# Two-pass feed-forward kernel behind windowed attention: 64-row matmul tiles for the later attention units, exponentials of the first batch from PSUM, and a new written order

## The chip, the cores and the metric

The kernel runs on one core of a Trainium2 chip. That core has five engines that run their own instruction streams and meet at semaphores: TensorE (PE, with its weight loads shown apart as PEld), VectorE (DVE), ScalarE (ACT), GpSimd (POOL) and SyncE (SP), whose queue issues nearly all of the DMAs here. The metric is the device time of one execution in microseconds. The kernel before takes 800.28 us, the median of three runs (800.1 to 801.37).

## What is computed

Four sequences of 576 tokens with 8 heads of 64 go through attention with a causal window: heads 0 to 3 see the last 32 tokens ("plain"), heads 4 to 7 every fourth of the last 128 ("dilated"). The result, 2304 tokens by 512, goes through a feed-forward layer and then through a second, gated one.

```python
rel = pos[:, None] - pos[None, :]
mask_plain = (rel >= 0) & (rel < window)
mask_dil = (rel >= 0) & (rel < window * dilation) & (rel % dilation == 0)
scores = np.where(masks[None, :, :, :], scores, -1000000000.0)
scores = scores - np.max(scores, axis=-1, keepdims=True)
attn = np.exp(scores)
attn = attn / (np.sum(attn, axis=-1, keepdims=True) + 1e-09)
...
h = x @ w_in                  # 512 -> 2048
x = (h - np.tanh(h)) @ w_out  # 2048 -> 512
a = x @ w1; b = x @ w2        # 512 -> 1024 each
out = (a * b @ w3) @ w_out2   # 1024 -> 1024 -> 512
```

Everything is float32. In the two feed-forward layers each operand is split into a high part of reduced precision (fp32r) and the rest, and three products of the parts make one product. The attention matmuls take float32 as it is; such a matmul stands in the trace as two records.

## The kernel before

**Units.** Attention is cut into 12 units: 4 batches times 3 groups of 3 query tiles of 64. A unit has two types, plain (`p`) and dilated (`d`), and a type has two pairs of heads; `e` is the pair, `h` the head within it. The tokens of the dilated heads are sorted by remainder on the host, so that both types see a band of 64 keys for each 32 queries. Units 0 to 2 are batch 0 ("first batch", `n < PB`); they go type by type. Units 3 to 11 are the later ones; their two types share one tile of two PSUM banks.

**Steps of a unit**, with the letters that the written order uses: `q` load keys and queries, `s` scores (`at_scores`, L508: a mask is laid into the bank by a bf16 matmul, L496, then 24 matmuls for each type contract all 128 rows, in which the queries of one head are followed by zeros for the other, into 32-partition strips), `M` maximum and subtraction on DVE (L526, L529), `E` exponential on ACT (L535), `N` sum and reciprocal on DVE (L541 to L546), `m` multiplication on POOL (L551), `T` three transposes for each type on PE (L561), `C` copies out of PSUM on ACT (L574: two for each type, each with a per-partition factor that keeps the rows of one head pair and zeroes the other's), `v` load values, `P` product with the values (`at_pv`, L592: 12 matmuls for each type, all 128 rows, 64 columns), `X` and `L` the high and low part into the activations X (ACT L614, DVE L619).

**The order.** `ORDER` is a table of words, one for each step of each unit, mixed with the steps of the first feed-forward group on a tile of tokens: `h` (L635), `t` tanh, `g`, `G`, `k` the split, `y` (L725), `Y` and `Z` evacuations; and with the preparation of weights: `w` load, `a`, `b`, `c` four bit operations that turn a float64 word into float32 (L144 on ACT; L149, L153, L159, L162 on DVE), `i`, `o` the split. The words are run through once and each engine gets its instructions in that order; nothing is reordered afterwards. Behind the table stand the other groups of the first layer, the second layer's weights and its products, none of which the change touches.

**Buffers.** The keys and queries of later units have three buffers each, one for a type of a unit; the values three; a weight waiting for conversion has two. A DMA on SP's queue is issued in the written order when its buffer is free and when the eighth DMA before it has landed.

Of the kernel before, what the change touches and what calls it, by code (L numbers as in the profile page):

```python
# [8 lines left out]
F32 = mybir.dt.float32  # L9
# [26 lines left out]
R = 4  # L36
# [13 lines left out]
K0 K1 q0p q1p s0p q2p q0d M0p q1d s1p E0p s2p s0d M1p N0p m0p w0 T0p E1p C0p N1p M2p q2d M0d E2p m1p  # L50
N2p T1p v0p s1d v1p m2p s2d w1 a0 E0d C1p T2p b0 P0p C2p N0d c0 M1d X0p M2d E1d v2p a1 m0d L0p b1
T0d q3p E2d P1p C0d w2 a2 q3d P2p N1d c1 m1d T1d s3 N2d C1d i0 m2d i1 T2d b2 c2 v0d v1d X1p L1p w3
P0d o0 X2p L2p o1 X0d i2 M3 P1d L0d X1d E3 a3 L1d q4p q4d h0 v2d s4 N3 C2d P2d w4 b3 t0 g0 h1 G0 c3
i3 X2d M4 t1 a4 m3p T3p k0 o2 L2d q5p E4 q5d g1 o3 y0 w5 h2 v3p q6p G1 s5 C3p v3d b4 c4 t2 k1 m3d
T3d g2 q6d i4 o4 a5 N4 C3d h3 m4p M5 t3 E5 b5 P3p c5 v4p T4p v4d C4p y1 N5 X3p L3p g3 P3d G2 X3d m4d
T4d i5 k2 C4d L3d s6 M6 q7p q7d o5 P4p v5p X4p L4p h4 t4 m5p y2 Y2 G3 E6 P4d X4d w6 g4 h5 T5p Z2 C5p
m5d s7 N6 G4 L4d v5d P5p k3 y3 t5 g5 a6 X5p G5 T5d C5d w7 k4 a7 b6 k5 v6p m6p L5p y4 h6 M7 q8p t6
T6p c6 g6 q8d y5 q9p C6p i6 h7 G6 v6d E7 b7 t7 c7 g7 P5d N7 k6 w8 G7 Y5 m6d s8 q9d X5d P6p X6p Z5
T6d k7 h8 v7p m7p y6 L5d C6d P6d t8 M8 a8 E8 g8 G8 q10p m7d h9 N8 m8p X6d v7d T7p C7p s9 T7d o6 k8
t9 g9 y7 C7d h10 M9 t10 L6p g10 T8p G9 v8p E9 i7 N9 b8 P7p L6d X7p w9 y8 h11 k9 m8d L7p Y8 q10d s10  # L60
q11p G10 t11 C8p m9p P7d g11 q11d Z8 X7d P8p X8p L7d L8p T8d k10 y9 G11 M10 h12 c8 y10 E10 k11 C8d
t12 v8d m9d v9p a9 v9d y11 w10 T9p C9p g12 h13 G12 P8d b9 Y11 k12 Z11 t13 N10 m10p g13 T9d m10d G13
s11 M11 P9p X8d L8d C9d X9p k13 c9 E11 y12 w11 T10p h14 y13 C10p T10d t14 g14 a10 b10 G14 P9d k14
N11 m11p L9p C10d v10p h15 t15 v10d y14 g15 G15 Y14 h16 v11p T11p t16 k15 Z14 g16 y15 X9d o7 L9d G16
k16 m11d P10p X10p h17 C11p c10 t17 v11d P10d g17 G17 y16 L10p X10d T11d C11d h18 a11 t18 P11p X11p
L10d L11p P11d k17 X11d w12 g18 y17 L11d Y17 b11 Q0 i8 G18 i9 c11 h19 Z17 k18 t19 o8 g19 h20 G19 h21
w13 t20 y18 k19 i10 y19 h22 g20 t21 g21 G20 G21 k20 i11 k21 y20 a12 h23 b12 o9 a13 b13 t22 g22 G22
o10 o11 Z20 k22 Y20 h24 c12 t23 c13 g23 i12 y21 G23 y22 o12 k23 i13 y23 t24 g24 G24 o13 k24 Z23 Y23
# [12 lines left out]
def attn_moe_kernel(  # L81
# [362 lines left out]
    def load_v(n, parts=AB):  # L444
        if n < NU:
            b, g = units[n]
            for ty in parts:
                v = v_home(n).rearrange("p (h t c) -> p h t c", h=2, t=TU)
                for e in range(2):

                    for t0, t1 in ((0, 1), (1, TU)) if g == 0 else ((0, TU),):
                        src = vt[b, 2 * ty + e, :HW, TU * g + t0:TU * g + t1].rearrange("k t c -> k (t c)")
                        ap = [list(d) for d in src.ap]
                        step = ap[0][0] * window(TU * g + t0, 1)
                        nc.sync.dma_start(
                            out=v[e:128:2, :, t0:t1].rearrange("k h t c -> k h (t c)"),
                            in_=bass.AP(tensor=src.tensor, offset=src.offset, ap=[ap[0], [step, 2], ap[1]]),
                        )
                vs[n, ty] = v
# [8 lines left out]
    def bank_of(n, ty):  # L468

        if n >= PB:  # L470
            return ust[n]["both"][:, ty]
# [706 lines left out]
```

## Time and profile before

| | |
|---|---|
| median of three runs | 800.28 us |
| profiled execution: own time | 802.01 us |
| its span, first to last instruction | 800.2 us |
| PE busy in the span | 779.9 us (97%) |
| DVE, ACT, POOL busy | 548.1, 292.8, 158.3 us |
| mean granted clock of TensorE | 0.994 |
| DMA, mean over the span | 144 GB/s; 298 GB/s in the first 37 us |

The profiled execution took 802.01 us and its instructions span 800.2 us of that. A busy PE is not PE at its peak: matmuls overlap in the array, so the duration of one record is longer than the distance between two. What a stretch of matmuls costs is read from the chain of work, where each piece lasts until the next one begins, and from counts of records in a window. The attention lies in the first 131 us; after that PE runs feed-forward matmuls until the end.

### The profile page before, as it was taken

The numbers are of one execution on the slowest core, as the hardware profiler recorded it, in microseconds if no ns is written. First come the engines' busy times: TensorE is split into PE (matmuls) and PEld (weight loads), VectorE is DVE, ScalarE is ACT, GpSimd is POOL, SyncE is SP. The second block draws the span as 40 slices with busy tenths as digits, with TensorE's granted clock in tenths as the row PEclk, the third lists the DMA queues.
The fourth block names the chain that finished last, engine by engine and source line by source line (L and its number), as shares of the span: only waits on it lengthen the run. The fifth ranks groups of instructions, "written<-read, shape, count | busy, mean of one in ns | idle before, by whom it ended". The sixth has DMA issues, their size and how long they took to land.

```text
span 800.2 us, 14174 instructions
## 1 busy us (share of the span) xinstructions
PE 779.9 (97%) x5592; PEld 688.0 (86%) x5592; DVE 548.1 (68%) x909; ACT 292.8 (37%) x546; POOL 158.3 (20%) x153
## 2 busy tenths in 40 slices
PE   5699999999999999999999999999999999999998
PEld 4589999888889888898888898799998999899996
DVE  4998675668888779987888889954454544734431
ACT  3566565443444444444444444321122111311111
POOL 3363343500022001210022223211121111211111
PEclk9799999999999999999999999999999999999999
DMA  9988742114455253632554344296203750156302
GB/s 300 302 247 294 236 155 73 53 53 126 150 160 158 105 162 116 186 119 66 156 155 136 105 134 131 93 340 211 93 1 115 238 187 1 41 181 202 118 1 79
DMA packets 62018, 115.58 MB, mean 144 GB/s; under 512 B 6400, under 2 KB 27008, under 8 KB 61952
## 3 DMA queue, kind: packets, MB, share of 16 engines
q1 hardware_dynamic: 61664, 114.32, 44.8%
q8 instruction: 44, 0.72, 0.4%
q10 hardware_dynamic: 288, 0.36, 0.2%
q14 instruction: 22, 0.18, 0.1%
HBM read 95.26 MB, written 19.40 MB: 143 GB/s over the span
## 4 chain that ended last, share of the span: by engine, by line
PE 89%; DVE 8%; ACT 1%; DMA 1%; issue 1%; ACTq 0%; SPq 0%; DVEq 0%
PE h L635 26%; PE y L725 25%; PE pr L979 22%; PE o L1042 6%; PE pr L1042 6%; PE x L592 2%; DVE a L159 2%; PE s L508 2%; DVE a L162 1%; DVE a L153 1%; PE t L561 1%; DVE a L149 1%; DVE Y L872 1%; DVE ms L541 1%; DMA id_sb<-in_ident 0%
## 5 line engine op out<-in xcount | busy, mean ns | idle before, releaser
L725 PE MATMUL y<-gs,LT 128*128 128x512 f32 (+1 forms) x520 | 121.9, 368 | 0.0
L725 PEld LDWEIGHTS y<-gs,LT 128*128 128x128 f32 x520 | 92.1, 188 | 16.3
L635 PE MATMUL h<-X,LT 128*128 128x512 f32 (+1 forms) x471 | 104.9, 370 | 0.0
L635 PEld LDWEIGHTS h<-X,LT 128*128 128x128 f32 x471 | 82.8, 188 | 15.2
L683 DVE TENSOR_TENSOR th<-h,th 128x512 f32<-128x512 f32 (+1 forms) x83 | 51.3, 618 | 58.5 <-ACT th L677 58.3
L979 PE MATMUL pr<-X 128*128 128x384 f32 x435 | 81.8, 334 | 0.0
L979 PE MATMUL pr<-X,LT 128*128 128x384 f32 x405 | 80.7, 336 | 0.0
L635 PE MATMUL h<-X,w 128*128 128x512 f32 (+1 forms) x381 | 78.8, 352 | 0.0
L677 ACT ACTIVATE th<-h 128x512 f32<-128x512 f32 (+1 forms) x83 | 44.8, 540 | 87.4 <-PE h L635 87.4
L979 PEld LDWEIGHTS pr<-X 128*128 128x128 f32 x435 | 76.2, 188 | 0.5
L159 DVE SCALAR_TENSOR_TENSOR a<-st,a 128x512 uint32<-128x512 uint32 x68 | 75.2, 1107 | 0.3
L979 PEld LDWEIGHTS pr<-X,LT 128*128 128x128 f32 x405 | 71.9, 188 | 1.3
L635 PEld LDWEIGHTS h<-X,w 128*128 128x128 f32 x381 | 62.8, 188 | 10.6 <-DVE th L683 0.2
L690 ACT ACTIVATE gs<-th 128x512 fp32r<-128x512 f32 (+1 forms) x83 | 47.9, 577 | 64.5 <-DVE th L683 57.5
L1016 DVE TENSOR_TENSOR u<-pr,u 128x384 f32<-128x384 f32 x72 | 40.1, 557 | 45.1 <-PE pr L979 38.5
L725 PE MATMUL y<-gs,w 128*128 128x256 f32 (+1 forms) x352 | 70.4, 330 | 0.0
L144 ACT ACTIVATE a<-st 128x512 f32<-128x512 f32 x68 | 45.5, 670 | 59.7 <-DMA st<-in_w 21.0
L992 ACT ACTIVATE cs<-u 128x384 fp32r<-128x384 f32 x24 | 12.6, 526 | 149.4 <-DVE u L1016 149.4
L1034 POOL TENSOR_TENSOR Y<-w,v 128x384 f32<-128x384 f32 x24 | 24.5, 1019 | 212.8 <-DVE w L1016 212.8
L725 PEld LDWEIGHTS y<-gs,w 128*128 128x128 f32 x352 | 54.6, 188 | 6.5
L162 DVE SCALAR_TENSOR_TENSOR a<-st,a 128x512 uint32<-128x512 uint32 x68 | 54.8, 806 | 2.3
L170 POOL TENSOR_TENSOR LT<-a,LT 128x512 fp32r<-128x512 f32 x18 | 25.8, 1436 | 152.2 <-ACT LT L167 152.2
(169 smaller groups left out, 1259.5 us busy)
## 6 DMA issues: line engine op xcount, KB each, us to landing
st<-in_w SPq DMA_DIRECT2D x28, 512.0 KB, 3.5
LT<-p SPq DMA_DIRECT2D x56, 256.0 KB, 4.2
X<-p SPq DMA_DIRECT2D x56, 256.0 KB, 4.7
st<-in_w_in SPq DMA_DIRECT2D x16, 512.0 KB, 4.2
st<-in_w_out SPq DMA_DIRECT2D x16, 512.0 KB, 4.1
q<-in_qz SPq DMA_DIRECT2D x18, 384.0 KB, 5.3
p<-LT SPq DMA_DIRECT2D x26, 256.0 KB, 4.5
v<-in_vt SPq DMA_DIRECT2D x32, 192.0 KB, 4.6
```

The lines of the kernel that those rows point to most:

```text
L144: nc.scalar.activation(out=a.bitcast(F32), in_=st[:, :, 1].bitcast(F32), func=ACTF.Abs)
L159: nc.vector.scalar_tensor_tensor(out=a, in0=st[:, :, 1], scalar=0xC0000000, in1=a, op0=ALU.bitwise_and, op1=ALU.bitwise_or)
L162: nc.vector.scalar_tensor_tensor(out=a, in0=st[:, :, 0], scalar=29, in1=a, op0=ALU.logical_shift_right, op1=ALU.bitwise_or)
L170: nc.gpsimd.tensor_tensor(out=lo, in0=a.bitcast(F32), in1=hi.bitcast(F32), op=ALU.subtract)
L635: nc.tensor.matmul(out=ps, lhsT=a[sel[0]], rhs=b[sel[1]], start=(start and i == 0), stop=(i == n - 1), **kw)
L677: nc.scalar.activation(out=th[:, :tn], in_=gst[i][:, :tn], func=ACTF.Tanh)
L683: nc.vector.tensor_tensor(out=th[:, :tn], in0=ps[:, :tn], in1=th[:, :tn], op=ALU.subtract)
L690: nc.scalar.activation(out=gs[:, 0, :tn], in_=th[:, :tn], func=ACTF.Copy)
L725: nc.tensor.matmul(out=y[k], lhsT=wt[sel[0]][:, 128 * k:128 * k + 128], rhs=gs[:, sel[1], tn * m:tn * m + tn], start=(cs[m] == 0 and n == ...
L979: nc.tensor.matmul(out=ps[:, :TP], lhsT=s[e][:, 128 * k:128 * k + 128], rhs=(hi, lo)[f][1][k], start=start and n == 0, stop=n == 5, skip_g ...
L1016: nc.vector.tensor_tensor(out=out, in0=ps[:, :TP], in1=x, op=op)
L1042: nc.tensor.matmul(out=tiles[m], lhsT=cs[e][:, 128 * m:128 * m + 128], rhs=WW[j][f], start=begin and n == 0, stop=end and n == 2,)
```

## The change

It has four parts.

1. The score matmuls of the later units contract the 64 rows of one head instead of 128 rows with zeros. There are as many as before (48 in a unit), each 64 columns wide, and each goes to a tile of 64 rows by 32 columns of the array: four strips for head 0, then four for head 1. The two banks of the unit now hold one head each, with the keys of both types side by side.
2. With that the transposes bring the dilated type to rows 0 to 63 and the plain one to rows 64 to 127. `C` of a later unit is one plain copy for each head instead of two with a factor. `P` takes both types at once: 48 matmuls of 64 rows by 64 columns, 32 columns wide, in four quarters of the array, instead of 24 of 128 rows and 64 columns wide. The values of a later unit are loaded pair by pair of heads into halves of the partitions, as many bytes in as many DMAs.
3. In the first batch DVE takes the negated maximum and multiplies it by 0.125. ACT then reads the scores from PSUM: six exponentials of 64 columns for each type with that maximum as bias, each of which also gives its sum. The subtraction (L529) and the sum (L541) on DVE go. The types of the first batch get other PSUM banks.
4. `ORDER` is a new table with the same words, in which `P` of a later unit is one word.

```diff
-K0 K1 q0p q1p s0p q2p q0d M0p q1d s1p E0p s2p s0d M1p N0p m0p w0 T0p E1p C0p N1p M2p q2d M0d E2p m1p
+q0p K0 K1 q1p s0p M0p w0 a0 b0 q2p E0p s1p M1p N0p q0d m0p w1 c0 q1d a1 s2p q2d b1 w2 c1 s0d T0p M2p
...
+    def scores_by_rows(n, g):
...
+                        for half in range(2):
+                            k0 = KS[t] - KS[TU * g] + window(t, half)
+                            j, c = 2 * e + half, QT * h + HQ * half
+                            nc.tensor.matmul(
+                                out=ps[HQ * j:HQ * j + HQ, h, i, 1 - ty], lhsT=q[r, e, i, c:c + HQ],
+                                rhs=k[r, e, k0:k0 + HW], start=False, stop=(i == TU - 1 and ty == 1),
+                                skip_group_check=True, tile_position=(64 * h, HQ * j),
+                            )
...
             nc.vector.tensor_reduce(
-                out=mx, in_=ps.rearrange("p u i k e -> p u i e k" if both else "p i k e -> p i e k"), axis=AX.X, op=ALU.max
+                out=mx, in_=ps.rearrange("p i k e -> p i e k"), axis=AX.X, op=ALU.max, negate=True
             )
-            nc.vector.tensor_tensor(
-                out=pm, in0=ps, in1=mx.unsqueeze(len(shape) - 2).to_broadcast(shape), op=ALU.subtract
-            )
+            nc.vector.tensor_scalar(out=mx, in0=mx, scalar1=0.125, scalar2=None, op0=ALU.mult)
...
+                    nc.scalar.activation(
+                        out=pm[:, i, :, e], in_=s["ps"][u][:, i, :, e], func=ACTF.Exp, scale=0.125,
+                        bias=s["mx"][:, u, at], accum_out=s["sm"][:, u, at],
+                    )
...
+            if n >= PB:
+                pb = ust[n]["pt"][u] = pb.rearrange("p i j e q -> p (i j e q)")[:, :TU * 128]
+                nc.scalar.activation(out=pb, in_=pt.rearrange("p i c -> p (i c)"), func=ACTF.Copy)
+                continue
...
+                            nc.tensor.matmul(
+                                out=x_part(n, ty, i, half, h)[:, e], lhsT=v[e][r, half, i, D * h:D * h + D],
+                                rhs=s["pt"][h][r, c:c + HQ], start=True, stop=True,
+                                tile_position=(r.start, 64 * h),
+                            )
```

Three places of the order bear on the prediction. The first is PE's stream from the products of the first batch to the scores of unit 5. Before (x48 are the scores of a unit, `v_104` and `v_105` the values of the first batch, L635 is `h`, L725 is `y`):

```order
L592 MATMUL x<-pb,v_104 64x2x32 x12
L635 MATMUL h<-X,WG 128x256 x12
...
L508 MATMUL s<-k,q 32x64 x48
L592 MATMUL x<-pb,v_105 64x2x32 x12
L635 MATMUL h<-X,WG 128x256 x12
L561 MATMUL t<-id_sb,pm 128x128 x3
L725 MATMUL y_746<-gs,WG 128x256 x6
L725 MATMUL y_747<-gs,WG 128x256 x6
L635 MATMUL h<-X,w_709 128x256 x8
...
L508 MATMUL s<-k,q 32x64 x48
```

Now the same stretch (L542 are the scores of a later unit, L699 is `h`, L789 is `y`, L650 is the product of a later unit, of which the first four matmuls stand here):

```order
L542 MATMUL s<-k,q 32x64 x48
L699 MATMUL h<-X,WG 128x256 x12
L657 MATMUL x<-pb,v_105 64x2x32 x12
L610 MATMUL t<-id_sb,pm 128x128 x3
L699 MATMUL h<-X,WG 128x256 x12
...
L789 MATMUL y_761<-gs,WG 128x256 x6
L789 MATMUL y_762<-gs,WG 128x256 x6
L650 MATMUL x<-pb,v 64x8x4 x2
L650 MATMUL x<-pb,v 64x32 x2
...
L542 MATMUL s<-k,q 32x64 x48
```

The scores of unit 4 have moved ahead of the first `h`, and the product of unit 3, both types in one, stands ahead of the scores of unit 5.

The second place is DVE's stream at the start. Before:

```order
L526 TENSOR_REDUCE ms<-s 128x6
L529 TENSOR_TENSOR pm<-s,ms 128x384
L526 TENSOR_REDUCE ms<-s 128x6
L529 TENSOR_TENSOR pm<-s,ms 128x384
L541 TENSOR_REDUCE ms<-pm 128x6
L545 TENSOR_SCALAR ms<-ms 128x6
L546 RECIPROCAL ms<-ms 128x6
```

Now (L561 and L564 are the negated maximum and its factor; L591 and L592 the end of `N`):

```order
L561 TENSOR_REDUCE ms<-s 128x6
L564 TENSOR_SCALAR ms<-ms 128x6
L149 TENSOR_SCALAR a<-a 128x512
L153 TENSOR_SCALAR a<-a 128x512
L561 TENSOR_REDUCE ms<-s_204 128x6
L564 TENSOR_SCALAR ms<-ms 128x6
L591 TENSOR_SCALAR ms<-ms 128x6
L592 RECIPROCAL ms<-ms 128x6
```

The two passes over 384 columns have gone from between the maxima, and the first weight's conversion stands there.

The third place is SP's queue behind the keys and queries of unit 4. Before (`k_591` and `q_592` are unit 4's dilated ones, `k_740` and `q_741` unit 5's, `v5` the last values of the first batch, `st` a weight):

```order
L432 DMA k_591<-in_kT 128x2x224
L435 DMA q_592<-in_qz 128x2x384
L455 DMA v5_105<-in_vt 64x2x384 x2
L139 DMA st_681<-in_w_out 128x1024
L432 DMA k_735<-in_kT 128x2x224
L435 DMA q_736<-in_qz 128x2x384
L432 DMA k_740<-in_kT 128x2x224
L435 DMA q_741<-in_qz 128x2x384
```

Now (`k_572` and `q_573` are unit 4's, `k_849` and `q_850` unit 5's, `v_742` and `v_775` the values of unit 3):

```order
L432 DMA k_572<-in_kT 128x2x224
L435 DMA q_573<-in_qz 128x2x384
L460 DMA v5_105<-in_vt 64x2x384 x2
L139 DMA st_614<-in_w_out 128x1024
L432 DMA k_724<-in_kT 128x2x224
L435 DMA q_725<-in_qz 128x2x384
L460 DMA v_742<-in_vt 64x2x128
...
L460 DMA v_775<-in_vt 64x2x256
L432 DMA k_849<-in_kT 128x2x224
L435 DMA q_850<-in_qz 128x2x384
```

The values of unit 3 now go ahead of the last keys and queries of unit 5.

## Rows read from the trace of the kernel before

**Rows 1.** The page: busy time of each engine over the span.
```profile
PE 779.9 (97%) x5592; PEld 688.0 (86%) x5592; DVE 548.1 (68%) x909; ACT 292.8 (37%) x546; POOL 158.3 (20%) x153
```

**Rows 2.** Stretches: length, busy PE, PEld, DVE, ACT, POOL, granted clock, DMA, GB/s.
```profile
0.00:37.00 37.00, 21.44 (x531) 16.75 (x531) 26.31 (x52) 15.14 (x31) 12.23 (x24) 0.89 0.93 298
37.00:60.00 23.00, 22.59 (x486) 20.14 (x487) 21.51 (x36) 15.24 (x31) 13.18 (x13) 0.95 0.83 259
60.00:80.00 20.00, 20.00 (x400) 18.63 (x399) 16.18 (x31) 12.95 (x30) 7.34 (x9) 1.00 0.89 294
80.00:100.00 20.00, 20.00 (x400) 18.63 (x399) 12.51 (x24) 11.08 (x25) 6.09 (x8) 1.00 0.74 237
100.00:131.00 31.00, 31.00 (x459) 29.48 (x459) 20.09 (x38) 19.64 (x45) 11.65 (x13) 1.00 0.43 131
```

**Rows 3.** Waits of PE up to 150 us: in total, times, longest.
```profile
PE s L496 <- DVE mask_sb L375: 5.7, 1, 5.7
PE x L592 <- DVE X L619: 4.0, 2, 2.6
PE t L561 <- POOL pm L551: 3.6, 3, 2.0
```

**Rows 4.** Timeline of PE, 30 to 48 us: start, us, instruction, idle before.
```profile
34.10 2.83 PE L592 MATMUL x<-pb,v 128*64 128x64 f32 x48 [2.55 <-DVE X L619]
36.85 2.83 PE L635 MATMUL h<-X,WG 128*128 128x256 f32 x12
...
39.96 1.55 PE L508 MATMUL s<-k,q 128*32 128x64 f32 x96
41.44 0.92 PE L592 MATMUL x<-pb,v 128*64 128x64 f32 x24
...
47.37 0.50 PE L496 MATMUL s<-mask_sb,id_sb 128*128 128x384 bf16 x2
```

**Rows 5.** Chain of work, 0 to 131 us: start, us until the next piece, what.
```profile
85.09 1.48 PE s L508 x96
...
88.46 1.44 PE h L635 x12
89.90 0.33 PE t L561 x3
90.23 0.85 PE x L592 x24
...
95.92 1.55 PE x L592 x48
```

**Rows 6.** Stretches of L508 alone: busy PE, PEld, granted clock, DMA, GB/s.
```profile
29.20:30.20 1.00, 1.00 (x50) 1.00 (x44) 0.50 0.89 281
85.30:86.30 1.00, 1.00 (x88) 1.00 (x80) 1.00 1.01 358
```

**Rows 7.** Timeline of SP's queue, 27 to 60 us: start, us, issue.
```profile
30.25 0.82 SPq L435 DMA_DIRECT2D q<-in_qz  x1
...
34.97 0.37 SPq L435 DMA_DIRECT2D q<-in_qz  x1
40.90 0.37 SPq L432 DMA_DIRECT2D k<-in_kT  x1
```

**Rows 8.** DMA issues up to 40 us: size, median us to landing.
```profile
q<-in_qz SPq DMA_DIRECT2D x5, 384.0 KB, 6.8
```

**Rows 9.** Groups of ACT by shape up to 60 us: busy us, mean ns, idle before.
```profile
L574 ACT ACTIVATE pb<-t,sel_sb 128x384 f32<-128x384 f32 x20 | 10.5, 577 | 5.6 <-PE t L561 3.9 <-PE x L592 1.8
...
L535 ACT ACTIVATE pm<-pm 128x768 f32<-128x768 f32 x3 | 2.5, 844 | 1.6 <-DVE pm L529 1.5
L535 ACT ACTIVATE pm<-pm 128x384 f32<-128x384 f32 x4 | 2.1, 521 | 7.1 <-DVE pm L529 7.1
```

**Rows 10.** Groups of DVE by shape up to 37 us: busy us, mean ns.
```profile
L529 DVE TENSOR_TENSOR pm<-s,ms 128x384 f32<-128x384 f32 x4 | 2.2, 557 | 0.1
L541 DVE TENSOR_REDUCE ms<-pm 128x6 f32<-128x384 f32 x4 | 2.1, 536 | 0.0
```

More of the change, by code (lines that the diff above doesn't have):

```diff
@@ L55 @@
[L55 to L64, printed above, removed]
@@ L444, in load_v @@
     def load_v(n, parts=AB):
[L445 to L457, printed above, removed]
-                        )
-                vs[n, ty] = v
+        if n >= NU:
+            return
+        b, g = units[n]
+        for part in parts:
+            v = v_home(n).rearrange("p (h t c) -> p h t c", h=2, t=TU)
+            for other in range(2):
+                if n < PB:
+                    rows, ty, e = slice(other, 128, 2), part, other
+                else:
+                    rows, ty, e = slice(HW * other, HW * other + HW), 1 - other, part
+                for t0, t1 in ((0, 1), (1, TU)) if g == 0 else ((0, TU),):
+                    src = vt[b, 2 * ty + e, :HW, TU * g + t0:TU * g + t1].rearrange("k t c -> k (t c)")
+                    ap = [list(d) for d in src.ap]
+                    step = ap[0][0] * window(TU * g + t0, 1)
+                    nc.sync.dma_start(
+                        out=v[rows, :, t0:t1].rearrange("k h t c -> k h (t c)"),
+                        in_=bass.AP(tensor=src.tensor, offset=src.offset, ap=[ap[0], [step, 2], ap[1]]),
+                    )
+            vs[n, part] = v
     NB = 2 * TU
@@ new lines, in at_max @@
+    def at_max(n, parts=AB):
+        s = ust[n]
+        if n >= PB:
+            ps = s["both"][:, :, :NB * HW].rearrange("p h (b k) -> p h b k", k=HW)
+            pm = s["pm"].rearrange("p h (b k) -> p h b k", k=HW)
+            nc.vector.tensor_reduce(out=s["mx"], in_=ps, axis=AX.X, op=ALU.max)
+            nc.vector.tensor_tensor(
+                out=pm, in0=ps, in1=s["mx"].unsqueeze(3).to_broadcast([128, 2, NB, HW]), op=ALU.subtract
+            )
+            return
+        for u in parts:
+            ps, pm = s["ps"][u], s["pm"][:, u].rearrange("p (i k e) -> p i k e", i=TU, e=2)
+            mx = s["mx"][:, u].rearrange("p (i e) -> p i e", e=2)
@@ L533, in at_exp @@
     def at_exp(n, parts=AB):
[L534 to L535 removed]
+        s = ust[n]
+        if n >= PB:
+            nc.scalar.activation(out=s["pm"], in_=s["pm"], func=ACTF.Exp, scale=0.125)
+            return
+        for u in parts:
+            pm = s["pm"][:, u].rearrange("p (i k e) -> p i k e", i=TU, e=2)
+            for i in range(TU):
+                for e in range(2):
+                    at = slice(2 * i + e, 2 * i + e + 1)
+                    nc.scalar.activation(
+                        out=pm[:, i, :, e], in_=s["ps"][u][:, i, :, e], func=ACTF.Exp, scale=0.125,
+                        bias=s["mx"][:, u, at], accum_out=s["sm"][:, u, at],
+                    )
@@ L546, in at_norm @@
-        nc.vector.reciprocal(out=sm, in_=sm)
+        for sm, pm in ([(s["sm"], s["pm"])] if n >= PB else [(s["sm"][:, u], s["pm"][:, u]) for u in parts]):
+            if n >= PB:
+                out, src = sm, pm.rearrange("p h (b k) -> p h b k", k=HW)
+            else:
+                out = sm.rearrange("p (i e) -> p i e", e=2)
+                src = pm.rearrange("p (i k e) -> p i e k", i=TU, e=2)
+            if n >= PB:
+                nc.vector.tensor_reduce(out=out, in_=src, axis=AX.X, op=ALU.add)
+            nc.vector.tensor_scalar(out=sm, in0=sm, scalar1=1e-9, scalar2=None, op0=ALU.add)
+            nc.vector.reciprocal(out=sm, in_=sm)
@@ L750, in spin @@
     def spin(n):
-        ps = h_tile()
+        ps = hA.tile([128, 512], F32, tag="h", name="h")
         for _ in range(n):
```

125 lines of the change are left out of this document (71 added, 54 removed).

## The prediction

> **What bounds the kernel now.** I read the page's busy times first: PE is busy for 97% of the span [rows 1], so time can be gained only where PE idles or where PE itself has less to do. The stretches say where. Up to 37 us PE is busy for 21.4 us only, with DVE at 26.3 and the DMA engines at 0.93 of their time, 298 GB/s; from 37 to 60 us PE has 22.6 of 23 us, DVE 21.5; from 60 us on PE is busy without a gap, and DVE and the DMAs fall back [rows 2]. The waits name the idle time at the start: the masks, then the chain of the first batch over DVE and POOL [rows 3]. So there are two regimes. Before about 40 us the first batch and the DMAs decide; from then to 131 us a microsecond taken off PE is a microsecond off the end, as long as operands arrive, and behind 131 us nothing changes.
>
> **Score and value matmuls (the main term).** First what a record costs, from the chain, where a piece lasts until the next begins. Three float32 transposes of 128 columns take 0.33 us, so a column takes 0.86 ns and 64 columns 55 ns [rows 5]. The 96 records of a unit's scores take 1.48 us, and two products in a row take 1.55 us for 48 records where one alone takes 0.85 for 24 [rows 5]. From the last two, starting a batch costs 0.15 us and a value record 29 ns; a score record costs (1.48 - 0.15) / 96 = 14 ns. Four score records make 55 ns and two value records 58 ns: the four strips, and the two halves, work side by side at the full column rate. Is it the array that limits, or the rate at which PE takes instructions? At half the granted clock a microsecond of scores shows 50 records against 88, those in flight at its ends counted in [rows 6]: the rate follows the array's clock, and at 14 ns no floor of the instruction rate shows yet.
>
> After the change a unit's 96 score records go to eight tiles: 12 rounds of 55 ns and the start, 0.81 us instead of 1.48. Its 96 value records are 32 columns wide in four quarters: 24 rounds of 27.5 ns plus the 3 ns by which the value rounds now exceed the column rate, and one start, 0.88 us instead of 1.70 (1.55 where the two products adjoin, as at 95.92; so in two of nine units). No row shows a 64-row tile. Bounds: nothing side by side beyond what there is (a record as dear as now, 35 ns for the values: 3.40 us a unit) and the figures above. I take those above, since at both clocks strips and halves already share the array without loss. Value products: 7 x 0.82 + 2 x 0.67 = 7.1 us. Scores: 0.67 us for units 5 to 11, 4.7 us; units 3 and 4 I leave out, for there PE waits for operands anyway.
>
> [...]
>
> **The copies.** `C` of a later unit goes from 2 x 577 ns to one copy of about 521 ns for each head [rows 9], 18 times: 11.4 us less of ACT, which is busy for 13 of the 20 us behind 60 us [rows 2]. PE hardly waits for it, so nothing; it is cover for the tighter pace. POOL's work, and DVE's for the later units, stay; the values come in as many DMAs. One wait is new: a value product now takes both of its PSUM banks at once, so it waits until DVE's last pass of the unit before has read them, and an `h` or `y` is queued behind it on PE. DVE is idle for 4 of the 20 us from 60 us on [rows 2], so I count nothing; without that cover it costs one pass of some 0.55 us [rows 10] a unit, 5 us in all, within the bounds of the last term.
>
> **The first batch.** DVE loses a subtraction of 557 and a sum of 536 ns for each of six types [rows 10], 6.6 us, and gets six passes over six columns, which cost between nothing and another 536 ns: 3.3 to 6.6 us less, I take 5. ACT pays. A copy with a per-partition factor takes 577 ns for 384 columns; 768 against 384 columns give 0.84 ns a column [rows 9]; so 64 columns with a pointer take 577 - 320 x 0.84 = 308 ns, six 1.85 us instead of 0.52. That is 8 us more of ACT on 15.1 in the first 37 us. What the sum adds, no row shows: bounds nothing and as much as the whole 384-column copy, 577 ns each, 17.6 us more. I take 308. The chain through one type stays as long (2 x 0.55 us gone from DVE, 1.3 come on ACT).
>
> So neither engine is full up to 37 us, and the DMAs decide when the scores of unit 4, which now stand ahead of the first `h`, can run. Ahead of the last of their operands SP issues ten pairs of keys and queries (5952 KB), four weights (2048), five value parts (1920) and the masks and identity (352), in both orders: 10.5 MB, 35 us at 298 GB/s [rows 2]. In the trace that query load is issued at 30.25 and takes about 6.8 us [rows 7, 8], 37 us. The scores then end at about 38. Before, scores of unit 4, first `h` and last first-batch product were done at 41.44 + 0.85 = 42.3 [rows 4, 5]; now 38 + 0.85 + an `h` of 1.44 (full clock [rows 5]) to 2.8 (low clock [rows 4]) = 40.3 to 41.6. Lead 0.7 to 2.0 us; I take 0.9, near the low clock, since PE idles before it as it does now.
>
> **Operands behind it.** The queue is held up before: it issues at 34.97 and next at 40.90, when a buffer comes free [rows 7]. That pause goes, but the values of unit 3 (768 KB) now go ahead of unit 5's last keys and queries: 2880 KB between the queries of units 4 and 5 instead of 2112. At 298 GB/s 2.95 MB take 9.9 us: unit 5 can begin at 47 us, where it began at 47.37 [rows 4]. PE would be there at 42.3 - 0.9 = 41.4, + two transposes 0.66 + `h` 1.44 + `y`, as long, 1.44 + values 0.88 = 45.8: a wait of 1.2 us. Up to unit 6 another 2048 KB, 7.0 us, against PE's 6.3 (masks 0.50 [rows 4], scores 0.81, two `h`, a `y`, two transposes 5.0): 0.7 us, and 0.6 for what I don't see. Later units have room: the DMA share is 0.74 and then 0.43 [rows 2]. So 2.5 us of new waits, 0 to 5.
>
> **Sum.** 7.1 + 4.7 + 0.9 - 2.5 = 10.2 us. The profiled execution took 802.01 us, its span 800.2 and 1.8 around it; that is 1.7 over the median of 800.28. 802.0 - 10.2 = 791.8 for an execution like that one, and 790.1 for the median, my forecast. Its own range: without new waits and with the whole lead, 13.8 us, 786.5; with 5 us of waits 792.6.
>
> **Rivals.**
> - *A small record costs what a large one does* (slower). Place: the value products. If a record of 32 columns on a quarter costs the 35 ns of today's, a unit pays 3.40 instead of 1.70 us: 15.3 us over nine units, less the lead of 0.9: 814.7. It decides above 17.7 ns a value record, where 96 of them cost today's 1.70. For it: no row shows fewer columns. Against: [rows 6], the rate follows the array's clock. [...] 8%.
> - *Row halves take turns.* Then scores stay at 1.48 and values cost 48 rounds of 30.5 ns and a start, 1.61 us: 9 x 0.09 + 0.9 = 1.7 us, 798.6. For it: the weights of both halves come through one stream of loads. 10%.
> - *Only one half of the gain.* Loading 64 columns of weights for every 32 columns streamed could hold the values at today's pace; then scores, lead and smaller waits leave 4.7 + 0.9 - 0.5, 795.2. A dear exponential (577 ns) comes out alike: ACT would be busy for 33 of the first 37 us, and if the first `h` is late by 5 us through it, 795.1. For the first: value rounds exceed the column rate now, score rounds don't. Together 25%.
> - The likeliest as summed: 57%.
>
> About 0.2%, 1.6 us, is what a measurement can tell from no change. Faster by more: the likeliest, the half gain and a part of the second rival: 0.85; within it 0.07; slower 0.08. The range for 8 times in 10: from 785, a little beyond the end without waits, to 798.6, where the row halves take turns.
>
> **What would show it.** Right: a unit's scores at 0.7 to 0.9 us and its values at 0.8 to 1.0 in the chain behind 50 us; the span shorter by 10 us by the end of the attention and by nothing behind it; short waits of PE for `q` or `k` at units 5 and 6. Wrong: scores still at 1.48 (row halves take turns), values above 1.70 (a floor for records), ACT without idle time before 37 us and the first `h` behind 40 us (dear exponentials), waits for operands that come again behind 60 us.

## The result and the profile after

| | before | changed |
|---|---|---|
| median | 800.39 us (beside the changed kernel's runs) | 810.21 us (807.67 to 813.71) |
| profiled execution, its span | 802.01, 800.2 us | 807.67, 805.9 us |
| PE busy, PE idle in the span | 779.9, 20.3 us | 778.3, 27.6 us |

The ratio is 1.0124, 95% interval 1.0076 to 1.0171: 1.2% slower, where the prediction was 790.1 us. The runs that tell most: the score tiles alone, with queries loaded without their zeros, take 799.36 us, a little less than before, and the change with value products on 128 rows and the same short queries 800.54. The changed kernel's profiled execution is the shortest of its four (to 813.71), and that of the kernel before is longer than any of its timed ones (801.37), so what the two profiles show covers 5.7 of the 9.8 us between the medians.

The page's engine line answers to [rows 1]: 432 matmuls and 432 weight loads more, and yet 1.6 us less of busy PE.

```profile
PE 778.3 (97%) x6024; PEld 686.4 (85%) x6024; DVE 540.5 (67%) x903; ACT 290.3 (36%) x594; POOL 155.1 (19%) x153
```

The stretches (columns as in [rows 2]) show where time went: between 37 and 60 us PE is busy for 19.43 us where it was 22.59, at a clock of 0.84 for 0.95, and of the three stretches behind, all full before, only one still is.

```profile
0.00:37.00 37.00, 20.70 (x507) 15.52 (x509) 19.43 (x47) 23.11 (x96) 11.50 (x24) 0.87 0.95 315
37.00:60.00 23.00, 19.43 (x423) 17.75 (x422) 17.57 (x29) 11.04 (x24) 10.26 (x10) 0.84 0.73 197
60.00:80.00 20.00, 18.77 (x563) 17.01 (x565) 12.85 (x25) 9.60 (x23) 7.54 (x9) 1.00 0.90 249
80.00:100.00 20.00, 20.00 (x534) 18.67 (x521) 15.03 (x27) 10.67 (x25) 5.96 (x8) 1.00 0.96 255
100.00:131.00 31.00, 28.84 (x574) 27.61 (x574) 19.28 (x36) 14.38 (x35) 13.00 (x15) 1.00 0.56 146
```

The waits of PE up to 150 us answer to [rows 3]. The kernel before has no wait for "issue" there, this one 10.4 us of it in seven pieces. "issue" is time in which PE had nothing to wait for that the profile names.

```profile
PE s L502 <- DVE mask_sb L375: 5.4, 1, 5.4
PE s L502 <- ACT pm L576: 4.8, 1, 4.8
PE s L542 <- issue: 3.6, 2, 2.8
PE x L657 <- issue: 2.3, 1, 2.3
PE y L789 <- issue: 1.4, 1, 1.4
PE t L610 <- issue: 1.2, 1, 1.2
PE x L657 <- ACT pb L625: 1.1, 1, 1.1
PE x L650 <- issue: 1.1, 1, 1.1
PE s L514 <- DMA Y<-in_qz: 1.0, 1, 1.0
PE h L699 <- issue: 0.8, 1, 0.8
```

PE's timeline shows the longest: PE stops in the middle of one run of like matmuls, after 56 of 96 score records, on operands that it was already using. A second stands inside unit 4's value product, after 62 of 96.

```profile
46.92 1.60 PE L650 MATMUL x<-pb,v 64*64 64x32 f32 x96
48.46 0.50 PE L527 MATMUL s<-mask_sb,id_sb 128*128 128x384 bf16 x2
48.89 0.79 PE L542 MATMUL s<-k,q 64*32 64x64 f32 x56
52.48 0.90 PE L542 MATMUL s<-k,q 64*32 64x64 f32 x40 [2.80 <-issue]
53.32 2.93 PE L699 MATMUL h<-X,w 128*128 128x256 f32 x12
56.04 0.84 PE L610 MATMUL t<-id_sb,pm 128*128 128x128 f32 x3
56.54 2.35 PE L789 MATMUL y<-gs,w 128*128 128x256 f32 x12
...
63.62 1.13 PE L650 MATMUL x<-pb,v 64*64 64x32 f32 x62
65.87 0.77 PE L650 MATMUL x<-pb,v 64*64 64x32 f32 x34 [1.12 <-issue]
```

Count between the two stops: 40 scores, `h` 12, `t` 3, `y` 12, `h` 12, `t` 3, 2 masks, 96 scores, `h` 12, 62 values: 254 records, and each is two instructions of PE, a weight load and a matmul: 508. From the stop before it (at 39.63, inside unit 4's scores) to 49.68 it is 253 records, 506. If a few waiting instructions of PE's sequencer are counted with them, that is twice 256. The profile's page shows what comes in such pieces. Its line on DMA queue 8 (packets, MB, share) has 16 KB a packet; for 256 instructions that would be 64 bytes each. PE's instructions over the packets are 12048 / 47 = 256 here, and 11184 / 44 = 254 in the kernel before.

```profile
q8 instruction: 47, 0.77, 0.4%
```

By these counts queue 8 brings PE's instructions in blocks of 256, which is an inference. At the ends of such blocks PE stands for up to 2.8 us here; the kernel before, with 44 packets, has no wait for issue.

The packets' own times in the trace close the chain. At six of the seven stops PE goes on 1.3 to 1.7 us after a packet of queue 8 has landed; at the longest, from 49.68 to 52.48 us, the packet starts at 49.81 and lands at 51.06. The seventh, the one of 1.2 us ahead of `t`, has no such packet (the last one landed 8 us earlier) and stands between two runs of matmuls: it is something else, so 9.2 of the 10.4 us are waits for instructions.

The chain shows what a unit's scores and products now take, against [rows 5]: 1.10 us for 1.48, and 1.53 for 1.70.

```profile
83.75 1.53 PE x L650 x96
...
88.93 1.10 PE s L542 x69
```

The first batch's exponentials (ACT groups up to 60 us, columns as in [rows 9]) are two instructions each, 339 to 398 ns for the pass and 228 to 287 for the sum.

```profile
L576 ACT ACTIVATE pm<-s,ms 128x64 f32<-128x64 f32 x24 | 7.1, 339 | 0.0
...
L576 ACT ACTIVATION_READ_ACCUMULATOR pm<-s,ms 128x1 f32 x24 | 5.5, 228 | 0.0
...
L576 ACT ACTIVATE Y<-s,ms 128x64 f32<-128x64 f32 x12 | 3.7, 398 | 0.0
L576 ACT ACTIVATION_READ_ACCUMULATOR Y<-s,ms 128x1 f32 x12 | 3.3, 287 | 0.0
```

**The difference of the two profiled spans, 5.7 us, as a sum.** Stops +10.4. Other waits of PE: 15.8 before ([rows 3] and two of 1.3 and 1.2), 12.7 now (the rows above and one of 0.4): -3.1. The head gets no shorter by it: two of the stops lie there (1.2 and 2.3), and up to 37 us PE idles for 16.3 us where it idled for 15.6. The longest new wait, 4.8 us, is for ACT's exponentials (`pm`, L576). Scores -3.4 (nine units at 0.38), values -1.2 (15.0 to 13.8). The rest, +3.0, is slower matmul time. Most of it follows the longest stop: PE idles for 2.8 us, and from 52.50 to 58.90 the granted clock is 0.56, where it is 1.00 from 60 us on; an `h` there takes 2.86 us in the chain for 1.43, and compared piece by piece that stretch loses 2.7 us.

### The profile page after: what moved, and what is told of

It is laid out like the page before. It is cut to its first block, busy times and chain, and to the rows that moved or that the text cites. A ratio compares the mean times of both kernels' runs of the same rounds, so it can differ in the third digit from the quotient of the medians.

```text
span 805.9 us, 15055 instructions
## 1 busy us (share of the span) xinstructions
PE 778.3 (97%) x6024; PEld 686.4 (85%) x6024; DVE 540.5 (67%) x903; ACT 290.3 (36%) x594; POOL 155.1 (19%) x153
## 4 chain that ended last, share of the span: by engine, by line
PE 91%; DVE 4%; DMA 2%; issue 1%; ACT 1%; SPq 0%; POOL 0%; ACTq 0%; POOLq 0%
PE h L699 26%; PE y L789 25%; PE pr L1043 22%; PE o L1106 6%; PE pr L1106 6%; PE x L650 2%; PE s L542 1%; DVE a L159 1%; PE t L610 1%; DMA st<-in_w_in 1%; DVE a L162 1%; PE x L657 1%; DVE Y L936 1%; DMA Y<-in_qz 1%; DVE a L149 0%
## 5 line engine op out<-in xcount | busy, mean ns | idle before, releaser
L789 PE MATMUL y<-gs,LT 128*128 128x512 f32 (+1 forms) x520 | 121.9, 368 | 0.0
L789 PEld LDWEIGHTS y<-gs,LT 128*128 128x128 f32 x520 | 92.0, 188 | 16.3
L699 PE MATMUL h<-X,LT 128*128 128x512 f32 (+1 forms) x471 | 104.9, 370 | 0.0
L699 PEld LDWEIGHTS h<-X,LT 128*128 128x128 f32 x471 | 82.8, 188 | 15.2
L699 PE MATMUL h<-X,w 128*128 128x512 f32 (+1 forms) x381 | 80.3, 357 | 0.8 <-issue 0.8
L159 DVE SCALAR_TENSOR_TENSOR a<-st,a 128x512 uint32<-128x512 uint32 x68 | 74.1, 1089 | 0.3
L699 PEld LDWEIGHTS h<-X,w 128*128 128x128 f32 x381 | 64.0, 192 | 11.3 <-issue 1.0
L789 PE MATMUL y<-gs,w 128*128 128x256 f32 (+1 forms) x352 | 71.1, 332 | 0.0
L789 PEld LDWEIGHTS y<-gs,w 128*128 128x128 f32 x352 | 55.3, 191 | 6.6
L162 DVE SCALAR_TENSOR_TENSOR a<-st,a 128x512 uint32<-128x512 uint32 x68 | 52.5, 772 | 2.4
```

The source lines that it names most:

```text
L159: nc.vector.scalar_tensor_tensor(out=a, in0=st[:, :, 1], scalar=0xC0000000, in1=a, op0=ALU.bitwise_and, op1=ALU.bitwise_or)
L162: nc.vector.scalar_tensor_tensor(out=a, in0=st[:, :, 0], scalar=29, in1=a, op0=ALU.logical_shift_right, op1=ALU.bitwise_or)
L699: nc.tensor.matmul(out=ps, lhsT=a[sel[0]], rhs=b[sel[1]], start=(start and i == 0), stop=(i == n - 1), **kw)
L789: nc.tensor.matmul(out=y[k], lhsT=wt[sel[0]][:, 128 * k:128 * k + 128], rhs=gs[:, sel[1], tn * m:tn * m + tn], start=(cs[m] == 0 and n == ...
```

## The experiments

Theories at the start: **F**, PE uses up its instructions faster than the next come; **O**, the new order and the exponentials on ACT cost, not the tiles. Later runs speak of **G** (F, with the order's part in it) and **T** (row tiles cost by themselves). "Stops" are PE's waits for issue, read from the one profiled execution of each run. The edits are shown in part, lines of `ORDER` too.

**e1_no_tiles.** Later units as before, new order and first batch kept.

```diff
...
-        if n >= PB:
-            scores_by_rows(n, g)
-            return
...
```

> The new written order and the new first batch stay; the later units' scores, copies, value loads and value products are as in the kernel before (128 rows). Theory F (the short matmuls on 64-row tiles use up PE's instructions faster than transfers bring new ones, and PE then stands in the middle of a run of like matmuls with nothing to wait for but issue): at most 1 us of such stops behind 35 us, values 1.55 to 1.70 us a unit, scores 1.48, time 798 to 802 us. Rival O (the new order and the exponentials on ACT are what costs, the tiles don't): 806 to 814 us.

803.96 us, ratio 1.0049 (1.0031 to 1.0067). Behind 35 us there are still two stops, 4.3 us. F expected at most 1 us, O 806 or more: neither fits. The order has a part in the stops.

**e2_half_values.** Half of the value records.

```diff
-                                out=x_part(n, ty, i, half, h)[:, e], lhsT=v[e][r, half, i, D * h:D * h + D],
-                                rhs=s["pt"][h][r, c:c + HQ], start=True, stop=True,
...
+                            out=x_part(n, ty, i, half, h), lhsT=v[0][r, half, i, D * h:D * h + D],
+                            rhs=rhs[:, :, half], start=True, stop=True, tile_position=(r.start, 64 * h),
```

> The changed kernel with half of the value records of a later unit: one matmul of 64 columns (both pairs of heads) with the first pair's values as weights in place of two of 32 columns; so the second pair's result is computed with the first pair's values. All else stays. If loading 64 columns of weights for each record sets the pace of the values, a unit's go from 1.53 to about 0.85 us (6 us over nine units). Theory F adds that most of the 9.1 us of PE's stops at issue go too, since 432 records fewer are to be brought: 790 to 795 us. Rival O: the stops stay, 800 to 803 us.

802.44 us, 1.0024 (1.0007 to 1.0041). The chain has one of these products as

```profile
82.12 0.86 PE x L649 x48
```

48 records of 64 columns in 0.86 us, 96 of 32 columns in 1.53: less a start of 0.15 us it is 15 and 14 ns a record, whether 32 or 64 columns are streamed. So the columns streamed don't set the pace of the 32-column records. What both have alike is the load of 64 columns of weights. That fits, but no run changes the load alone. A fixed time per record is the rival: against it, score records with 32 columns of weights take 10 ns. On one tile four times 14 ns is 58 ns, and e8 below has records with 32 columns of weights 26 ns apart on one tile (192 in 4.96 us, at a granted clock of 1.00), though in bf16. Stops behind 35 us fell from 6.9 to 5.0 only, and the time, 7.8 us below the changed kernel, missed the 790 to 795 us of F.

**e3_shift32.** 32 short matmuls ahead of everything.

```diff
+        for _ in range(SHIFT):
+            nc.tensor.matmul(out=ps[:, :8], lhsT=warm[:, :128], rhs=warm[:, :8], start=True, stop=True)
```

> The changed kernel with 32 matmuls of 8 columns ahead of everything on PE, while PE is idle. Theory F: the stops come where a block of 256 PE instructions ends, so each moves by 32 records toward the program's start in the stream of matmuls (the one after 56 of the 96 score records of unit 5 comes after some 24 of them), and the sum of stops changes with what stands at the block ends: 798 to 815 us, places tell. Rival O (a wait on an engine or a DMA that the profile doesn't name): the stops stay at the same matmuls, 806 to 814 us.

810.95 us, 1.0127 (1.0098 to 1.0156). The timeline of PE:

```profile
49.71 0.44 PE L543 MATMUL s<-k,q 64*32 64x64 f32 x24
52.22 1.34 PE L543 MATMUL s<-k,q 64*32 64x64 f32 x72 [2.07 <-issue]
...
63.84 0.66 PE L651 MATMUL x<-pb,v 64*64 64x32 f32 x30
65.59 1.23 PE L651 MATMUL x<-pb,v 64*64 64x32 f32 x66 [1.09 <-issue]
```

After 24 instead of 56 scores, after 30 instead of 62 values: both moved by just 32 records. The stops hang on the count of instructions, not on what the matmuls wait for.

**e4_q_half.** Queries of later units without their zero columns.

```diff
-                q = home(n, 2 * TU * 2 * QT, "kv", "q")
+                wide, src = (2, qz) if n < PB else (1, qh)
+                q = home(n, 2 * TU * wide * QT, "kv", "q")
```

> The changed kernel with the later units' queries loaded without their zero columns: 3.5 MB less of DMA of the attention's 28 MB; the matmuls are the same. Theory F with transfers that are late because the DMA engines are full: the stops get shorter, but stay at the same matmuls, 799 to 807 us. Rival D (the stops are only the DMA engines' load, or waits for keys and queries): they go, and the time is 794 to 798 us.

805.64 us, 1.0086 (1.0057 to 1.0114). Behind 35 us 6.6 us of stops stay; the one in unit 5's scores is at the same place, after 56 records, 2.0 us for 2.8.

```profile
47.44 0.79 PE L544 MATMUL s<-k,q 64*32 64x64 f32 x56
50.19 0.66 PE L544 MATMUL s<-k,q 64*32 64x64 f32 x40 [1.97 <-issue]
```

With 3.5 MB less to load the stops stay in place. Whether more load makes them longer isn't shown by one execution each.

**e5_v128, e6_v128_spaced, e7_spaced.** e5: value matmuls on 128 rows, both types in one. e7: six words of the order moved apart. e6: both.

```diff
-                                out=x_part(n, ty, i, half, h)[:, e], lhsT=v[e][r, half, i, D * h:D * h + D],
-                                rhs=s["pt"][h][r, c:c + HQ], start=True, stop=True,
+                            out=x[:, 2 * i + half], lhsT=v[e][:, half, i, D * h:D * h + D],
+                            rhs=s["pt"][h][:, i, 2 * e + half].rearrange("p a q -> p (a q)"),
...
-t4 g4 P4 y2 X4p
+t4 g4 y2 P4 X4p
```

> The changed kernel with its score tiles, but each value matmul of a later unit again on all 128 rows: the keys of both types lie above each other, the copies out of PSUM write zeros for the other type's rows, and one matmul of 64 columns serves both types. 48 value records in a unit instead of 96, so 192 PE instructions (weight loads and matmuls) fewer out of some 510. Theory G (PE stops where 256 instructions are used up in less time than the next 256 take to come, some 4 us or more while the DMA engines are full; the new order, which puts value products next to scores, makes such places, and short records make more of them): values 1.55 to 1.70 us, scores stay at 1.10, stops at issue behind 35 us 2 to 5 us instead of 8.3, time 796 to 803 us. Rival T (64-row tiles themselves slow PE): no better than the changed kernel, 806 or more.

> As the run with 128-row values, and in the written order six words moved so that scores and value products of later units stand at least one h or y farther apart (scores of units 5 and 11 later, value products of units 4, 7 and 8 behind the next y). Theory G: stops at issue behind 35 us at most 2 us, 792 to 798 us, the fastest so far. Rival T: 806 or more. If the stops hang on the load of the DMA engines alone they stay as without the moves.

> The changed kernel with the same six words moved and nothing else. Theory G: the stop in unit 5's scores (2.8 us) gets shorter by one to two, those behind 100 us go, stops behind 35 us 3 to 6 us, time 800 to 807 us. If the order of the words has no part in it, the stops stay at 8 us or more and the time at 806 to 814.

810.09, 809.75 and 810.22 us; 1.0117 (1.0090 to 1.0144), 1.0116 (1.0101 to 1.0131), 1.0116 (1.0093 to 1.0139). All three expectations missed. Stops behind 35 us are 6.4, 2.7 and 7.9 us, against 6.9 in the changed kernel (not 8.3, as the expectation has it): moving six words alone removed no stops in sum, and where e6 did get rid of most of them its time didn't follow. Two things ate that: the stretch behind the attention, from the `h` of step 25 to the last matmul, takes 642.1 us in e5 and 642.2 in e6, where it is 639.0 to 639.1 in the changed kernel and in e1 to e4, and e6 waits 1.4 us for DVE before an `h`.

**e11_v128_spaced_pad.** e6 with its new constant at another size.

```diff
-    half_sb = const.tile([128, 2], F32, name="half_sb")
+    half_sb = const.tile([128, 32], F32, name="half_sb")
```

> The run with 128-row values and the six moved words once more; the only difference is that its constant (the selector of the row halves) is 128 bytes of a partition long instead of 8, so that all that lies behind it in SBUF moves by 120 bytes. In the earlier run the stretch behind the attention was 3.1 us longer than in all others, with 231 ns between matmuls on weights in w where the others have 229. If the place in SBUF is the reason: 229 ns again, and 806 to 807.5 us. If not: 809 to 811 us.

807.88 us, 1.0089 (1.0074 to 1.0104), between its two expectations; the stretch behind the attention 641.0 us. So 1.2 of e6's 3.2 us follow the size of the constant, and with it where the tiles lie in SBUF; the other 2.0 stay unexplained.

**e8_burst.** The kernel before with 256, 256 and 768 matmuls of 8 columns.

```diff
+        for _ in range(n):
+            nc.tensor.matmul(
+                out=ps[:32, :8], lhsT=warm[:, :32], rhs=warm[:, :8], start=True, stop=True, skip_group_check=True
+            )
```

> The kernel before with three bursts of matmuls of 8 columns that wait for nothing: 256 behind the scores of unit 6 (DMA engines full), 256 behind h of step 20 (DMA share 0.4), 768 in the product of w3 and w_out2. Each is 2 instructions. Theory G: at the first one to two stops at issue of 1.5 to 4 us where the kernel before has none, at the second stops of 0 to 2 us, and in the third a stop for each 128 matmuls, so that 256 instructions take 3 to 4.5 us. Rival: the matmuls follow each other at 10 to 30 ns without a stop; then instructions come fast enough and something else stops PE in the changed kernel.

One run, 844.6 us. The bursts in PE's timeline, the first behind unit 6's scores (from 58 us on), the second behind `h` of step 20, the third in the product of w3 and w_out2, behind its first 445 matmuls:

```profile
57.85 1.34 PE L483 MATMUL s<-warm 128*32 128x8 bf16 x47
60.30 3.58 PE L483 MATMUL s<-warm 128*32 128x8 bf16 x128 [1.11 <-issue]
64.31 0.35 PE L483 MATMUL s<-warm 128*32 128x8 bf16 x7 [0.42 <-issue]
...
142.78 4.96 PE L483 MATMUL h<-warm 128*32 128x8 bf16 x192
148.06 1.85 PE L483 MATMUL h<-warm 128*32 128x8 bf16 x64 [0.32 <-issue]
...
533.79 3.57 PE L483 MATMUL h<-warm 128*32 128x8 bf16 x128 [0.26 <-issue]
537.51 3.57 PE L483 MATMUL h<-warm 128*32 128x8 bf16 x128 [0.15 <-issue]
541.52 1.95 PE L483 MATMUL h<-warm 128*32 128x8 bf16 x67 [0.43 <-issue]
```

Stops in a kernel that had none, and from the first stop of a burst on, one after every 128 matmuls, that is 256 instructions; from one resumption to the next it is 3.7 to 4.0 us, 14 to 16 ns an instruction. The start of a burst goes without one: the third runs 445 matmuls (890 instructions) in 11.72 us before its first stop, so some instructions lie ready. The first burst's stops, 1.1 and 0.4 us, are shorter than the 1.5 to 4 us expected; with the clock granted at 0.50 these matmuls themselves take 3.6 us for 256 instructions. A unit of the changed kernel has 192 in 1.10 us (scores) and 192 in 1.53 (values).

**e9_old_order_tiles, e10_old_order_v128.** The tiles in the old order and first batch, the two value words of a unit made one; in e10 with the value matmuls of e5. The order's edit is shown against the kernel before, the middle of one line.

```diff
-E5 b5 P3p c5 v4p T4p v4d C4p y1 N5 X3p L3p g3 P3d G2 X3d
+E5 b5 c5 v4p T4p v4d C4p y1 N5 g3 P3 X3p L3p G2 X3d
```

> The kernel before, with its first batch (subtraction and sum on DVE) and its written order, but the later units on 64-row tiles as in the changed kernel (scores, copies, values; the two value words of a unit become one, behind the later of them, and a few words of units 5, 7 and 8 move for it). Theory G (PE stops where 256 instructions are used up before the next 256 have come): the tiles save 0.38 us of scores and 0 to 0.17 us of values a unit, 3.4 to 5 us, and bring stops at issue of 3 to 6 us behind 35 us, for value products still stand next to scores in places: 798 to 804 us. Rival O (what costs is the new order with the new first batch, in some way that has nothing to do with the tiles): no stops, 795 to 797 us. Rival T (tiles cost by themselves): 806 or more.

> As the run with the old order and tiles, but value matmuls on 128 rows that serve both types, 192 PE instructions a unit fewer, and the small constant that this needs takes 128 bytes of a partition instead of 8. Theory G: stops behind 35 us at most 2 us, scores 1.10, values 1.55 to 1.70: 796 to 800 us, the first that isn't slower than the kernel before. Rival T: 803 or more.

821.57 and 819.59 us. They don't answer the question: the joined product comes so late that the next unit's copy overwrites its operand first (the words `C4p`, `C10p` and `C11p` stand ahead of `P3`, `P9` and `P10`, and there are two such buffers), so in three units other probabilities are multiplied, and that the value buffers are held; PE waits 4.5 us (e9) and 8.0 us (e10) for queries and values behind 35 us. So no run has value products on 64 rows in the old order.

**e12_order_only.** The new order, all else as before but the first batch's banks.

```diff
-K0 K1 q0p q1p s0p q2p q0d M0p q1d s1p E0p s2p s0d M1p N0p m0p w0 T0p E1p C0p N1p M2p q2d M0d E2p m1p
+q0p K0 K1 q1p s0p M0p w0 a0 b0 q2p E0p s1p M1p N0p q0d m0p w1 c0 q1d a1 s2p q2d b1 w2 c1 s0d T0p M2p
...
-        return banks0["s"][:, m % 2]
+        return banks0["s"][:, m // 3]
```

> The new written order alone, with the banks of the first batch that it needs: later units on 128 rows, first batch with subtraction and sum on DVE as before. The run without tiles took 803.96 us with the exponentials from PSUM. If the order makes the stops (theory G): stops of PE at issue as in that run, 5 to 8 us in all, and 803 to 807 us. If the exponentials on ACT are the cost: 799 to 801 us.

804.52 us, 1.0048 (1.0027 to 1.0070). In the new order the product of unit 3 (both types) stands next to unit 5's scores, and a stop follows without any row tile:

```profile
45.86 1.62 PE L592 MATMUL x<-pb,v 128*64 128x64 f32 x48
47.41 0.50 PE L496 MATMUL s<-mask_sb,id_sb 128*128 128x384 bf16 x2
47.84 1.55 PE L508 MATMUL s<-k,q 128*32 128x64 f32 x96
49.32 0.97 PE L635 MATMUL h<-X,w 128*128 128x256 f32 x6
52.55 1.65 PE L635 MATMUL h<-X,w 128*128 128x256 f32 x6 [2.27 <-issue]
```

The order alone costs 4.0 us. Its trace has 3.3 us of stops, less than the 5 to 8 expected, and waits for loads (2.7 us for values, 2.2 for queries of the first batch) where the kernel before waits for DVE and POOL. In sum PE idles no longer, 20.4 us for 20.3; what is longer by 2.4 us is its busy time (782.3), and behind the stop six matmuls of `h` take 1.65 us where six take 0.97 ahead of it.

**e13_score_tiles, e14_score_tiles_wide.** Old order and first batch; scores on row tiles, with a pair of heads in each row half so that copies and value products stay.

```diff
+                                out=ps[HQ * j:HQ * j + HQ, e, 1 - ty, i], lhsT=q[r, h, i, HQ * half:HQ * half + HQ],
+                                rhs=k[r, h, k0:k0 + HW], start=False, stop=(i == TU - 1 and ty == 1),
+                                skip_group_check=True, tile_position=(64 * e, HQ * j),
```

> The kernel before with one edit: scores of later units on 64-row tiles. The two rows halves hold the two pairs of heads (not the two heads of a pair as in the changed kernel), each row half writes its own PSUM bank, and DVE's subtraction puts the columns back in the old layout, so copies, value products and the written order stay as before. Queries come without zero columns (3.5 MB less). Theory G: scores 1.10 us instead of 1.48 a unit, no stop at issue over 1 us since value products stay spread out: 796 to 798.5 us. Rival T (row tiles bring stops or something of their own): 800 or more.

> The same with queries loaded as long as before (half of each is zeros that nothing reads), so the DMAs move what they moved. Theory G: PE bounds the units from 40 us on, the loads have room: within 1 us of the run with short queries, 796 to 799 us. If the smaller loads were the gain: 799.5 to 801 us.

799.36 us, 0.9984 (0.9975 to 0.9993), the version that beats both kernels; 800.08 us, 0.9993 (0.9985 to 1.0002), no change that can be told. Both missed G's range, and e14 lies where the smaller loads were to be the gain: they may be half of it, but the two intervals overlap and this isn't settled. T is out for the scores: e13 has no stop, and its chain shows scores at 1.10 and values by type.

```profile
83.27 1.10 PE s L542 x70
...
88.02 0.85 PE x L636 x24
```

Nine times 0.38 would be 3.4 us; the medians differ by 1.3. The two profiles differ by more than the medians, 797.3 us of span for 800.2: PE is busy for 3.6 us less (776.3) and idles for 0.7 more, 0.6 of it in the waits for the first batch's products (DVE, L663). The profiled execution of the kernel before is 1.3 us above the median that stands beside e13.

**e15_score_tiles_exp, e16_new_order_score_tiles.** e13 with the new first batch, as below; e13's scores in the new order and first batch (the edits of e1 and e13 together).

```diff
+                        nc.scalar.activation(
+                            out=s["pm"][:, u, i, :, e], in_=s["ps"][u][:, i, :, e], func=ACTF.Exp, scale=0.125,
+                            bias=s["mx"][:, u, at], accum_out=s["sm"][:, u, at],
+                        )
```

> The score tiles of e13 in the old written order, and the first batch with the maximum as bias, six exponentials from PSUM a type and sums in the same pass. DVE loses 6.6 us, ACT gains some 8 (estimate from 577 and 844 ns copies); PE waits for POOL and DVE in the first 37 us (7 to 8 us in the kernel before) can shrink by 1 to 3 us or grow as ACT falls behind. If the new first batch is harmless: 797 to 799.5 us. If the exponentials cost: 801 to 805.

> The new written order and first batch of the run without tiles (803.96 us), with the score tiles and short queries of e13; values by type on 128 rows. Theory G: 9 x 0.38 us less of scores and 3.5 MB less of loads against somewhat more stops, since the value products stand next to scores: 800 to 803 us, above e13. If the order costs nothing once the value records are few: 797 to 799.

801.21 us, 1.0007 (0.9998 to 1.0015), and 800.54 us, 1.0005 (0.9994 to 1.0016). The new first batch makes e13 slower by 1.9 us, and with it come waits for issue that e13 has not:

```profile
PE t L625 <- POOL pm L615: 4.2, 4, 1.8
PE t L625 <- issue: 2.8, 2, 1.6
PE x L656 <- DVE X L683: 1.1, 1, 1.1
```

The two waits for issue stand ahead of `t`, as the one of 1.2 us in the changed kernel does, which isn't a stop of the kind above. What ends them isn't shown. In the new order the new first batch costs nothing that can be told: e1, which has it, took 803.96 us, e12, which hasn't, 804.52.

e16 against e1: score tiles and short queries take off 3.4 us. e16 against e4, which have the same order, first batch and short queries: value products on 64 rows, with the copies and the layout they need, cost 5.1 us by the medians (6.5 by the ratios). That is the largest cost of a part measured here (the order 4.0, the first batch 1.9 or nothing). Behind 35 us e4 has 6.6 us of stops, e16 one:

```profile
PE h L699 <- issue: 1.0, 1, 1.0
```

## Why the prediction was wrong

- **What bounds the kernel.** Right that PE sets the end from 40 to 131 us and that nothing changes behind 131: from the `h` of step 25 both kernels take 639.0 us. The step that failed by most is the next one: the prediction asked whether the rate of instructions limits, and answered from [rows 6] that no floor of it shows, so its sum has nothing for it. Those rows lie inside one unit's scores, 192 instructions, and can't show what a block of 256 costs. It cost 9.2 us of stops and most of 3.0 us of slower matmuls behind them.
- **The sum, term by term** (spans of the two profiles). Forecast: values -7.1, scores -4.7, lead -0.9, new waits +2.5, stops and slower matmuls nothing: -10.2. Measured: values -1.2, scores -3.4, other waits -3.1, no new waits for operands, stops +10.4, slower matmuls +3.0: +5.7.
- **Value products, the largest term (-7.1).** 1.53 us a unit, not 0.88; -1.2 in all. This is the step that failed as worked out. I let the columns streamed set the pace and put the loads of weights among the rivals (the first half of "only half of the gain"). e2 shows that the columns streamed don't set it, and fits the loads.
- **Scores (-4.7).** The mechanism was right in part: eight tiles do share the array, but not without loss. The size was 0.38 us a unit for 0.67. A record costs (1.10 - 0.15) / 96 = 10 ns, not 7, and a round of eight 79 ns, not 55; why is not shown.
- **The price of many short records.** The slower rival put it at the array (35 ns a record) and was wrong in that: 14 ns. The price is in bringing them: with 192 instructions in 1.10 us and 192 in 1.53, PE is through a block before the next one has come. Shown by e3 (the places move with the count), e8 (a stop after every 256 instructions, 3.7 to 4.0 us from one to the next), the count of records between stops (254 and 253) and the packets that land 1.3 to 1.7 us ahead of the resumptions. 9.2 us, and some 2.7 us of low clock (0.56) behind the longest. That the rival's 814.7 us lie near the measured 810.2 is luck.
- **The written order.** I took the new table as free but for the queue. e12: by itself it costs 4.0 us. It lets value products and scores adjoin, and e12's stop of 2.3 us lies there; that this place makes up the whole 4.0 us is not shown.
- **First batch.** I took 308 ns an exponential; with the instruction that reads the sum it is 567 to 685, at and above the upper bound that I had (577). e15 prices the new first batch at 1.9 us in the old order. The lead of 0.9 us didn't come: the product that I put at 41.4 ended at 43.3, behind three waits for issue of 4.2 us in all and a wait of 4.8 us for the exponentials. Of the signs named, the first `h` behind 40 us came true (40.8), ACT without idle time did not (busy for 23.1 of 37 us).
- **New waits for operands (+2.5).** They didn't come: no wait of PE for a later unit's keys or queries is among the rows.

What stays open: why a block sometimes comes late and sometimes not at like load of the DMA engines; the runs of one kernel differ by 6 us (807.67 to 813.71), which fits stops that depend on such chance, but that was not measured. Also open are the 4.1 us by which the medians differ more than the profiled executions, and why e7 gained nothing from the words moved apart.

## What to carry to other kernels

Where matmuls are short, count PE's instructions as well as its time: here PE stopped for up to 2.8 us with units of 192 instructions in 1.10 us and 192 in 1.53, in e8 after each 256 instructions, which took 3.7 to 4.0 us with the stop, and the place shows as "issue" inside a run of like matmuls. Splitting a matmul into smaller tiles paid most where the number of weight loads stayed the same: the scores (48 matmuls before and after) went from 1.48 to 1.10 us, the value products, with twice as many, from 1.70 to 1.53, and each load more is an instruction to bring. And a new order of the work is a change of its own: run it alone.

## What the runs showed of the hardware

- Instructions of PE in the bursts of e8, from the first stop of a burst on: 3.7 to 4.0 us for 256, even where the DMA engines had little to do (0.03 of their time between 541 and 543 us, at a granted clock of 0.50). In the changed kernel PE went on from six of its seven waits for issue 1.3 to 1.7 us after a packet of 16 KB had landed on queue 8.
- Records that load 64 columns of weights: 14 ns each in four quarters of the array (changed kernel, 1.53 us for 96), 29 ns each in two column halves over 128 rows (e5: 1.55 us for 48). Four records, one in each quarter, take 58 ns. That the loads set this pace fits, but was not shown.
- An exponential that also gives its sum is two instructions on ACT, 339 to 398 and 228 to 287 ns for 64 columns, where one of 384 columns without a sum took 521 [rows 9].
- With a constant of 8 bytes a partition ahead of the large tiles the part behind the attention took 642.2 us (e6), with one of 128 bytes and all else the same 641.0 us (e11).
